# The last group's output in two token halves, its squares on two engines, and the first scores by halves

## The chip, the cores and the metric

The kernel runs on one core of one Trainium2 chip. The metric is the device time of one execution in microseconds; where several runs were made, their median is given. TensorE is the matrix engine, VectorE and ScalarE the two elementwise engines (DVE and ACT in the profile), GpSimd (POOL) issues the transfers that cast or add. "The trace" is the record of every instruction of one profiled execution, and "the profile" what is read from it. Its span, from the first to the last instruction of the program, is some 1.8 us shorter than the device time of the same execution.

## The reference

Four batches of 6080 tokens with 256 channels go through an attention between channels, and the result, 24320 tokens, through two linear layers with a squared relu between them:

```python
def _attn_ref(q, k, v, tau):
    qn = q / (np.linalg.norm(q, axis=1, keepdims=True) + 1e-06)
    kn = k / (np.linalg.norm(k, axis=1, keepdims=True) + 1e-06)
    s = kn.transpose(0, 2, 1) @ qn / tau          # 256 x 256 scores of each batch
    s = s - s.max(-1, keepdims=True)
    a = np.exp(s)
    a /= a.sum(-1, keepdims=True) + 1e-09
    return (v @ a).astype(np.float32)

def _moe_ref(x, w_in, w_out, s, b):               # x: 24320 x 256, d_ff = 2048
    r = np.maximum(x @ w_in, 0.0)
    return ((s * (r * r) + b) @ w_out).astype(np.float32)
```

## The kernel before

The attention matrix is folded into the first layer's weights, batch by batch. So the main stream is: for each group of 512 tokens sixteen steps, each a first-layer product into PSUM; a relu on ScalarE every second step; squares; and the second layer. For most groups the second layer is a scheme of seven products (`seven_items`) on sums S of the squares, run one group behind. The first and the last group use the plain second layer. The last group has 256 tokens, two rows of tokens per partition.

```python
def plain_mm2(g, m):                      # output of one group, slice m of the hidden units
    for h in range((nj + 1) // 2):        # one pass for the last group
        js = [j for j in (2 * h, 2 * h + 1) if j < nj]
        if m == 0:
            o_plain[g, h] = ps_o.tile([P, 2, C], FP32, tag="o_ps", name="o_ps")
        ...                               # for j in js: one matmul of 256 columns
        if m == FT - 1:
            ...
            evacuate(o_sbs[g][:, js[0] : js[-1] + 1, :], o, rowconst, 1)
            if js[-1] == nj - 1:
                store(g)
```

The scores of the first batch are needed before the main stream can start; a softmax without the maximum is taken of their transpose:

```python
po(nc.vector.tensor_mul(                  # recip(): scale by the norms, 512 per partition
    st["s"], self.s_ps, st["r"][:, 1, :, None].broadcast_to((P, CH, C))))
...
for j in range(CH):                       # turn(): four transposes on TensorE
    for ch in range(CH):
        po(nc.tensor.transpose(
            st["t"][:, j, ts(ch, P)], st["s"][:, ch, ts(j, P)], ident32))
```

## Time and profile before

| | before |
|---|---|
| time, median of the first 3 runs | 724.11 us (724.01 to 724.62) |
| span of the profiled run | 722.44 us |
| TensorE, VectorE, ScalarE busy | 97%, 86%, 75% |
| first matmul after the wait for w_in | 40.33 us |
| tail: from the last group's first matmul of 256 columns (703.20) to the end | 19.24 us |

The tail: everything of the change but the first scores lies in it. It starts here (start, length, engine, line, what):

```profile
703.20 0.38 PE L572 MATMUL h_ps<-vT,wa 128*128 128x256 f16 x2
```

The stretches of 0.2 us add what no instruction shows, the data of the last store. The columns are the stretch, its length, busy time of TensorE, its weight loads, VectorE, ScalarE and GpSimd with their instructions, the granted clock, the share of the DMA engines that was busy, and GB/s:

```profile
719.80:720.00 0.20, 0.00 (x0) 0.00 (x0) 0.00 (x0) 0.00 (x0) 0.00 (x0) 1.00 1.07 410
720.20:720.40 0.20, 0.00 (x0) 0.00 (x0) 0.00 (x0) 0.00 (x0) 0.00 (x0) 0.57 0.67 246
```

All engines are idle and the transfer runs at 410 GB/s; with the stretches beside these, it moves data for about 0.8 us (0.82 by the records of its packets).

### The profile page before, as it was taken

How to read it: one execution, taken by the hardware profiler on the slowest of the kernel's cores; microseconds unless marked ns; L12 is line 12 of the kernel's file. 1: busy time of each engine (PE TensorE's matmuls, PEld its weight loads, DVE VectorE, ACT ScalarE, POOL GpSimd, SP SyncE). 2: the span in 40 equal slices, each digit the busy share in tenths (PEclk: the TensorE clock that was granted, in tenths of full speed). 3: DMA queues.
4: the chain of work that ended last, by engine and by line, in shares of the span. 5: the costliest groups of instructions: out<-in, count | busy, mean ns of one | idle time of the engine just before them, and what ended most of it. 6: DMA issues, size and time to landing. Idle time of an engine off the chain costs nothing.

```text
span 722.4 us, 17620 instructions
## 1 busy us (share of the span) xinstructions
PE 700.5 (97%) x7486; PEld 505.8 (70%) x7486; DVE 623.9 (86%) x873; ACT 541.8 (75%) x585; POOL 112.0 (15%) x191
## 2 busy tenths in 40 slices
PE   4799999999999999999999999999999999999997
PEld 2556777766777777777677777777668777777776
DVE  4779999988889999998788999998888888888886
ACT  4479877887777777788777778778777777877772
POOL 4522331211201222111010222111000000000000
PEclk9999999999999999999999999999999999999999
DMA  9999997556465979464863777836323333321201
GB/s 237 209 258 139 176 173 139 95 114 124 97 113 109 157 138 144 101 96 81 149 142 65 138 136 124 152 79 96 96 66 75 93 70 74 100 55 58 70 30 75
DMA packets 86303, 83.83 MB, mean 116 GB/s; under 512 B 56224, under 2 KB 61232, under 8 KB 86224
## 3 DMA queue, kind: packets, MB, share of 16 engines
q0 software_dynamic: 26176, 43.74, 37.6%
q1 hardware_dynamic: 59616, 37.64, 20.9%
q8 instruction: 59, 0.97, 0.6%
q10 hardware_dynamic: 432, 1.31, 0.5%
q14 instruction: 20, 0.16, 0.1%
HBM read 78.91 MB, written 24.90 MB: 144 GB/s over the span
## 4 chain that ended last, share of the span: by engine, by line
PE 88%; DMA 6%; issue 2%; DVE 1%; ACT 1%; POOL 1%; POOLq 0%; ACTq 0%
PE h_ps L572 43%; PE o_ps L716 38%; PE s_ps L142 4%; PE wa_ps L284 2%; DMA qk<-in_q_dram 2%; DMA w_in<-in_moe_w_in_dram 1%; DMA f<-f 1%; DMA qk<-in_k_dram 1%; ACT r L582 1%; PE o_ps L620 1%; POOL qk L126 1%; DVE o_sb L600 0%; DVE S L642 0%; ACT g L593 0%; PE t_ps L247 0%
## 5 line engine op out<-in xcount | busy, mean ns | idle before, releaser
L582 ACT ACTIVATE r<-h_ps 128x1024 f16<-128x1024 f32 (+1 forms) x384 | 387.8, 1013 | 147.6 <-PE h_ps L572 146.0
L572 PE MATMUL h_ps<-vT,wa 128*128 128x512 f16 (+7 forms) x1632 | 452.0, 365 | 0.6 <-ACT r L582 0.4
L716 PEld LDWEIGHTS <-S 128*128 128x128 f16 x2944 | 198.0, 98 | 85.1 <-DVE S L642 0.4
L716 PEld LDWEIGHTS <-g 128*128 128x128 f16 x2208 | 155.1, 98 | 74.1
L595 DVE TENSOR_TENSOR g<-r 128x2048 f16<-128x2048 f16 (+2 forms) x154 | 176.6, 1147 | 16.9 <-ACT r L582 16.5
L716 PE MATMUL o_ps<-T,S 128*128 128x128 f16 x2208 | 183.3, 219 | 0.3 <-DVE S L642 0.2
L572 PEld LDWEIGHTS <-wa 128*128 128x128 f16 x1632 | 136.1, 98 | 21.3 <-issue 1.0
L716 PE MATMUL o_ps<-w_out,g 128*128 128x128 f16 x1472 | 134.3, 219 | 0.3 <-DVE u L600 0.3
L600 DVE SCALAR_TENSOR_TENSOR o_sb<-o_ps,s_out,u 128x256 f32<-128x256 f32 x138 | 66.6, 482 | 50.3 <-PE o_ps L716 48.1
L593 ACT ACTIVATE g<-r 128x1024 f16<-128x1024 f16 x93 | 97.9, 1053 | 0.0
L142 PE MATMUL s_ps<-qk 128*128 128x256 f16 (+1 forms) x384 | 69.6, 281 | 14.5 <-ACT qk L133 7.0
L331 POOL DMA_DIRECT2D v<-in_v_dram x48 | 31.8, 670 | 243.5 <-DMA vT<-v 190.8
L188 POOL DMA_DIRECT2D f<-f x33 | 28.9, 875 | 244.7 <-DVE f L178 191.6
L600 DVE SCALAR_TENSOR_TENSOR u<-o_ps,s_out,rowconst 128x256 f32<-128x256 f32 x138 | 66.1, 479 | 0.5 <-PE o_ps L716 0.5
L716 PE MATMUL o_ps<-N,g 128*128 128x128 f16 x736 | 63.5, 219 | 0.0
L716 PE MATMUL o_ps<-w_out,S 128*128 128x128 f16 x736 | 63.5, 219 | 0.0
L165 ACT ACTIVATE sq<-qk 128x1024 f16<-128x1024 f16 (+3 forms) x49 | 50.4, 1033 | 10.7 <-DMA qk<-in_k_dram 7.5
L644 DVE TENSOR_TENSOR S<-S,g 128x2048 f16<-128x2048 f16 (+1 forms) x47 | 56.5, 1202 | 1.3
L642 DVE TENSOR_TENSOR S<-g 128x2048 f16<-128x2048 f16 (+1 forms) x47 | 56.1, 1193 | 0.0
L648 DVE TENSOR_TENSOR S<-g,S 128x2048 f16<-128x2048 f16 x46 | 56.0, 1218 | 0.0
L646 DVE TENSOR_TENSOR S<-g 128x2048 f16<-128x2048 f16 x46 | 55.9, 1216 | 0.0
L142 PEld LDWEIGHTS <-qk 128*128 128x128 f16 (+1 forms) x384 | 32.6, 101 | 20.2 <-DVE qk L132 8.9
(68 smaller groups left out, 321.8 us busy)
## 6 DMA issues: line engine op xcount, KB each, us to landing
out_dram<-o_sb SPq DMA_DIRECT2D x46, 512.0 KB, 3.1
v<-in_v_dram POOLq DMA_DIRECT2D x47, 256.0 KB, 4.7
qk<-in_k_dram POOLq DMA_DIRECT2D x42, 256.0 KB, 6.0
qk<-in_q_dram POOLq DMA_DIRECT2D x42, 256.0 KB, 7.5
f<-f POOLq DMA_DIRECT2D x30, 128.0 KB, 3.1
vT<-v SPq DMA_TRANSPOSE x182, 3.3
w<-in_moe_w_out_dram POOLq DMA_DIRECT2D x4, 512.0 KB, 11.9
raw<-in_q_dram ACTq DMA_DIRECT2D x2, 512.0 KB, 6.6
```

The source lines that it names most:

```text
L142: po(nc.tensor.matmul(self.s_ps[:, ch, :], kc[:np_, j, ts(ch, P)], qc[:np_, j, :], start=(c == 0 and j == 0 and ch == 0), stop=(c == len(s ...
L165: po(nc.scalar.activation(out=st["sq"][:np_, 1, js, :], in_=kc[:np_, js, :], func=AF.Square))
L572: po(nc.tensor.matmul(dst, wa[:, ci, ts(m, P)], src, start=(ci == 0), stop=(ci == CH - 1), skip_group_check=True))
L582: po(nc.scalar.activation(out=r16[:, :, i % 2, :n], in_=h_tiles.pop((g, i))[:, :, :n], func=AF.Relu))
L593: po(nc.scalar.activation(out=dst, in_=src, func=AF.Square))
L595: po(nc.vector.tensor_mul(dst, src, src))
L600: po(nc.vector.scalar_tensor_tensor(out=dst, in0=src, scalar=s_out, op0=ALU.mult, in1=add, op1=ALU.add))
L642: po(nc.vector.tensor_add(T[1], A21, A22))
L644: po(nc.vector.tensor_sub(T[2], T[1], A11))
L646: po(nc.vector.tensor_sub(T[3], A11, A21))
L648: po(nc.vector.tensor_sub(T[4], A12, T[2]))
L716: po(nc.tensor.matmul(st[name][:, j, :], a()[:, i, ts(j, P)], w[:, i, :], start=first, stop=last, skip_group_check=True))
```

## The change

Its intent is to shorten the end. The last group's output is computed for one half of the tokens first, so that this half's eviction and store lie under the other half's matmuls, and only half an eviction and half a store follow the last matmul. ScalarE takes every second square, to relieve VectorE. At the start, the first scores are scaled in two pieces, so that TensorE can turn the first piece early. The core of the diff:

```diff
-                po(nc.vector.tensor_mul(
-                    st["s"], self.s_ps, st["r"][:, 1, :, None].broadcast_to((P, CH, C))))
+                if self.b == 0:
+                    for ch in range(CH):
+                        po(nc.vector.tensor_scalar_mul(
+                            out=st["s"][:, ch], in0=self.s_ps[:, ch],
+                            scalar1=st["r"][:, 1, ch : ch + 1]))
+                else:
+                    ...                       # as before
@@ turn()
-                for j in range(CH):
-                    for ch in range(CH):
+                for ch in range(CH):
+                    for j in range(CH):
@@
+    def last_mm2(j, m):
+        g = NG - 1
+        if m == 0:
+            o_plain[g, j] = ps_o.tile([P, 2, C], FP32, tag="o_ps", name="o_ps")
+        o = o_plain[g, j][:, 0:1, :]
+        ...                                   # one matmul of 256 columns
+        if m == FT - 1:
+            ...
+            po(nc.vector.scalar_tensor_tensor(
+                out=o_sbs[g][:, j, :], in0=o[:, 0, :], scalar=s_out, op0=ALU.mult,
+                in1=rowconst, op1=ALU.add))
+            store(g, j, j + 1 if j == 0 else None)
@@ plain_mm2
+        if g == NG - 1:
+            last_mm2(0, m)
+            if m == FT - 1:
+                for i in range(FT):
+                    last_mm2(1, i)
+            return
@@ main loop, plain groups
-                square(g, m // 2, m // 2 + 1, nc.vector)
+                late = g > 0 and m // 2 % 2 == 1
+                square(g, m // 2, m // 2 + 1, nc.scalar if late else nc.vector)
```

More of the change, by code (lines that the diff above doesn't have):

```diff
@@ L239, in recip @@
                 st["s"] = sm_pool.tile([P, CH, C], FP32, tag="sm_s", name="sm_s")
-                po(nc.vector.tensor_mul(
-                    st["s"], self.s_ps, st["r"][:, 1, :, None].broadcast_to((P, CH, C))))
+                if self.b == 0:
[4 more added lines that the diff above has]
+                else:
+                    po(nc.vector.tensor_mul(
+                        st["s"], self.s_ps, st["r"][:, 1, :, None].broadcast_to((P, CH, C))))
             def turn():
                 st["t"] = self.bank("t_ps", CH, C)
-                for j in range(CH):
-                    for ch in range(CH):
+                for ch in range(CH):
+                    for j in range(CH):
                         po(nc.tensor.transpose(
@@ L609, in store @@
             in_=o_sb[:, j0:j1, :]))
+    def last_mm2(j, m):
+        g = NG - 1
+        assert group(g)[1] == 2
+        if m == 0:
+            o_plain[g, j] = ps_o.tile([P, 2, C], FP32, tag="o_ps", name="o_ps")
+        o = o_plain[g, j][:, 0:1, :]
+        po(nc.tensor.matmul(o[:, 0, :], g_tiles[g][:, m % 2, m // 2, ts(j, P)],
+                            w_out16[:, m, :], start=(m == 0), stop=(m == FT - 1),
+                            skip_group_check=True))
+        if m == FT - 1:
+            if j == 0:
+                o_sbs[g] = opool.tile([P, TG // P, C], FP32, tag="o_sb", name="o_sb")
+            po(nc.vector.scalar_tensor_tensor(
+                out=o_sbs[g][:, j, :], in0=o[:, 0, :], scalar=s_out, op0=ALU.mult,
+                in1=rowconst, op1=ALU.add))
+            store(g, j, j + 1 if j == 0 else None)
     def plain_mm2(g, m):
         _, nj = group(g)
+        if g == NG - 1:
[4 more added lines that the diff above has]
+            return
         for h in range((nj + 1) // 2):
```

## The prediction

> **What bounds the kernel now.** I read the page first (shares by engine, then the 40 slices), then the chain that ended last, and then only the two short stretches that the change touches: 35 to 42 us, where the first scores are scaled, and 703 us to the end, the last group of 256 tokens.
>
> ```profile
> PE 700.5 (97%) x7486; PEld 505.8 (70%) x7486; DVE 623.9 (86%) x873; ACT 541.8 (75%) x585; POOL 112.0 (15%) x191
> PE   4799999999999999999999999999999999999997
> ...
> PE 88%; DMA 6%; issue 2%; DVE 1%; ACT 1%; POOL 1%; POOLq 0%; ACTq 0%
> ```
>
> TensorE is full from the fourth slice to the last and makes 88% of the chain. Nothing in the change takes a matmul out: it can only move waits, and the few microseconds at each end when TensorE is not the bound. The chain of waits, around the first scores and at the end:
>
> ```profile
> 30.04 10.25 DMA w_in<-in_moe_w_in_dram
> 40.28 0.05 issue
> 40.33 1.04 PE wa_ps L284 x4
> ...
> 707.62 0.45 PE o_ps L716 x8
> 708.07 0.22 PE o_ps L620 x2
> 708.29 0.22 PE h_ps L572 x2
> 708.51 0.55 PE o_ps L716 x8
> 709.06 0.22 PE o_ps L620 x2
> 709.27 0.22 PE h_ps L572 x2
> 709.49 0.52 PE o_ps L716 x8
> ...
> 716.86 1.11 PE o_ps L620 x10
> 717.96 0.02 issue
> 717.99 0.75 DVE o_sb L600
> ```
>
> Columns are start, length, what. To be seen: the chain passes from the load of w_in (10.25 us) straight to a matmul at 40.33, so the scaling and turning of the scores at 36 to 37.5 us is not on it. In the last group one step is 0.22 (first layer, two matmuls of 256 columns) + 0.45 (eight products of the group before) + 0.22 (output, two matmuls) = 0.88 us; only two steps are longer, by 0.10 and 0.07. Then ten output matmuls, one eviction of 0.75 us and a store. The timeline of the tail and of the scores:
>
> ```profile
> 36.02 0.69 DVE L240 TENSOR_TENSOR sm_s<-s_ps,rnrm 128x512 f32<-128x512 f32 x1
> 36.85 0.63 PE L247 MATMUL t_ps<-ident,sm_s 128*128 128x128 f32 x4 [0.16 <-DVE sm_s L240]
> 37.52 0.84 ACT L257 ACTIVATE eT<-t_ps,rnrm 128x256 f16<-128x256 f32 x2 [0.53 <-PE t_ps L247]
> ...
> 715.78 0.60 ACT L582 ACTIVATE r<-h_ps 128x512 f16<-128x512 f32 x1 [1.17 <-PE h_ps L572]
> 716.41 0.42 DVE L595 TENSOR_TENSOR g<-r 128x512 f16<-128x512 f16 x1 [0.58 <-ACT r L582]
> 716.89 0.48 DVE L600 SCALAR_TENSOR_TENSOR o_sb<-o_ps,s_out,rowconst 128x256 f32<-128x256 f32 x1
> 717.99 0.75 DVE L600 SCALAR_TENSOR_TENSOR o_sb<-o_ps,s_out,rowconst 128x512 f32<-128x512 f32 x1 [0.61 <-PE o_ps L620]
> 718.77 0.35 ACTq L607 DMA_DIRECT2D out_dram<-o_sb  x1
> ```
>
> After 718.77 no compute engine works. The stretches of 0.2 us show the last store's data moving from about 719.6 to 720.4 (297, 410, 358, 246 GB/s); the span ends at 722.4, some 2 us later.
>
> **What the Trainium skill says.** (1) "TensorE: Matmul & The Clock Gate", section Back-to-back issue gap: 256 columns take 262 cycles at 2.4 GHz, an estimate from it of 109 ns. The trace agrees: 0.22 us for two, 1.11 for ten. (2) "ScalarE: Activation LUTs", section What ACT_TABLE_LOAD costs: 186 ns + 0.833 ns per element with immediate scale, about 93 ns of it overlapped by the next. For 512 elements that is 612 ns; the trace has 594 as the mean of the 128x512 relu, so I take 0.60 us for a square on ScalarE. (3) "VectorE: DVE Perf Modes", section The TRN2 errata: a fixed extra cost per instruction, so small tiles pay relatively more. The trace agrees: the eviction costs 0.48 us for 256 elements and 0.75 for 512, not half. (4) "DMA: Bandwidth & Descriptors", section Latency and other measured facts: a DMA has a fixed cost of about 2 us, dominated by the receipt from memory. The last store landed 2.1 us after issue, about 0.8 of it data.
>
> **The change part by part.**
> *First scores by halves.* One 0.69 us multiply becomes two on 256 elements. The 256-element PSUM multiply on VectorE elsewhere in this stretch took 0.48 us, and one such instruction starts about 0.40 after another (evictions at 698 to 717 us). So the first half is ready at 36.02 + 0.48 = 36.50, the second at 36.02 + 0.40 + 0.48 = 36.90 (now 36.71). Five filler matmuls hold TensorE to about 36.53. With the lag of 0.14 us now seen, the first two turns start at 36.64, the last two at 37.04, and the last ends near 37.43 in place of 37.48. The exponentials gain 0.05 us; but at 40.33 TensorE waits for w_in with 0.16 us of idle time before it, so this gain is swallowed: 0.
>
> *Squares shared.* Eight squares of 128x512 on VectorE (0.42 us each, 0.33 start to start) become four there and four on ScalarE (0.60 us). ScalarE idles 1.17 us in nearly every pair of steps, so it has room. VectorE is freed of 4 x 0.33 = 1.3 us of its queue. Its queue is what made the two long steps: the partial sums S for the other group's products (ending 709.33) and the eviction that frees a bank (ending 708.39) are followed 0.06 us later by the products at 709.39 and 708.45. Without the square at 706.98 both come 0.33 us earlier: 709.00 and 708.06.
>
> *Two halves.* The number and width of matmuls are the same, 32 of 256 columns. Before the end, each step now has one output matmul, not two, so a step is 0.77 us and TensorE asks earlier. I step through it. Step 7's products would start at 708.45 - 0.10 - 2 x 0.11 = 708.12; the bank is free at 708.06 + 0.06 = 708.12: no wait. Step 8's would start at 708.89, the sums come at 709.06: a wait of 0.17. Steps 9 to 12 find their inputs (the third sums are ready at 710.53, wanted at 711.36). Step 13's are wanted at 712.90; VectorE's fourth sums end at 712.86, so about 0.02. Step 15 starts at 714.24, the last group's products end at 715.44.
>
> Then comes the new end. The five remaining matmuls of the first half start at 715.44; the fourth needs the last square. Last first-layer result 714.62, relu 714.66 to 715.26, square on ScalarE 715.30 to 715.90, seen at 715.96, wanted at 715.77: a wait of 0.19. The second half takes a new PSUM tile. Of the three buffers of that pool, two hold the other group's accumulators and one the first half, so it must take the oldest accumulator, which VectorE evicts from 715.64 to 716.12: free at 716.18, just when the first half's last matmul has been issued (715.96 + 0.22). No further wait. Sixteen matmuls of 0.108 end issuing at 717.91 and, with the drain of 0.17 seen now, finish at 718.08, against 717.95 now. So the waits rise from 0.17 to about 0.38 us; the extra 0.2, less rounding, costs about 0.13.
>
> What is won is behind it. The last eviction is 0.48 in place of 0.75: -0.27. The first half's eviction and store lie under the second half's 1.7 us of matmuls. The last store is 128 KB, not 256: at the 410 GB/s seen, 0.64 us of data becomes 0.32; with rows of 1 KB rather than 2 KB a little of it is lost (packet records of the trace: 4 KB 160 ns, 2 KB 86 ns, so by straight line 49 ns for 1 KB, and 8 x 37 = 0.30 us saved per queue engine). The fixed receipt stays. Sum: 0 + 0.13 - 0.27 - 0.30 = -0.44, rounded to -0.5 since the waits at 709 and 715.8 are worked from rounded lags and may be smaller. 724.11 - 0.5 gives 723.6 us.
>
> **The rivals.** (a) *The waits are larger*: the square on ScalarE lies on the way to the end (it is 0.18 us longer than on VectorE), and the second half's tile waits for an eviction. If either slips by some 0.4 us, the gain is eaten: 724.1. For it: the three-buffer pool and the serial relu, square, matmul; against it: both releases fall within 0.2 us of their need in my working. (b) *The waits vanish*: VectorE, relieved, delivers its sums in time, and the 0.17 us of old waits go without new ones; then the end is at 717.8 and the whole is -0.9: 723.2. For it: 1.3 us of VectorE time freed; against it: TensorE's demand moves up by 0.11 a step as well. (c) *The store is all fixed cost*: only the eviction counts and the total is -0.1: 724.0. Against it: data was seen moving for 0.8 us. (d) *The start counts*: if the w_in load lands earlier in most runs than in the profiled one, the scores would be on the path, worth 0.05 us or, if the second half's later multiply dominates, costing as little. Not seen in this trace.
>
> **Range and chances.** The rivals lie between 723.2 and 724.1; the three runs before spread over 0.6 us, and loads at the start vary from run to run. I give 722.9 to 724.3. 2% is 14.5 us; the whole stretch after the last group's start is 19 us and nearly all of it matmuls, so neither verdict beyond 2% is plausible: 0.005 faster, 0.985 within, 0.01 slower.
>
> **What would show it.** In the new profile: TensorE's matmul after the w_in load still near 40.3 with slightly more idle time before it; in the last group, output matmuls one at a time with steps of 0.77 us, four 128x512 squares of about 0.6 us on ScalarE, the long step at 709.06; a gap of about 0.2 us before the fourth of the first half's last five; sixteen output matmuls ending near 718.1; a final eviction of 0.48 us; and last store data lasting about 0.4 us. Wrong would be: a shift of the matmul at 40.3 us by more than 0.2, any change between 60 and 700 us (there is no changed instruction there), a gap over 0.5 us before the second half, or an end that does not move though the eviction and the store shrank.

## More of the kernel before

The experiments ran in sets, on two chips; times are compared only within a set.

For the batches after the first, the squares of q and k that make the norms are folded per chunk, and each chunk's fold is added to the first chunk's by an accumulating transfer. Matmuls with ones then sum over the partitions; their result shares a PSUM bank with an accumulator of the second layer.

```python
def into_first():
    dst, src = self.rows[0][0][:np_], st["f", 1][:np_]
    po(nc.gpsimd.dma_start(out=dst, in_=src, accum_op=ALU.add))
```

## The result, and the profile after

The changed kernel took 724.26 us (723.56 to 724.57, 6 runs), the kernel before 724.44 us (724.01 to 725.0, 6 runs). The ratio is 0.9996, with a 95% interval of 0.9983 to 1.0009: the same. Ratios here are the mean time of one kernel's runs over that of the other's of the same rounds, so not quite the ratio of the quoted medians. All runs with rounds were fast ones, the granted clock 0.998 to 1.0.

Seen from the time, the change did next to nothing. The trace says otherwise.

**The start.** The timeline of the changed kernel:

```profile
35.82 0.87 DVE L242 TENSOR_SCALAR sm_s<-s_ps,rnrm 128x256 f32<-128x256 f32 x2
36.45 0.74 PE L253 MATMUL t_ps<-ident,sm_s 128*128 128x128 f32 x4
37.23 0.84 ACT L263 ACTIVATE eT<-t_ps,rnrm 128x256 f16<-128x256 f32 x2 [0.43 <-PE t_ps L253]
40.13 1.04 PE L290 MATMUL wa_ps<-w_in,eT 128*128 128x512 f16 x4 [0.24 <-DMA w_in<-in_moe_w_in_dram]
```

From the start of the scaling to the exponentials are 37.23 - 35.82 = 1.41 us; before they were 37.52 - 36.02 = 1.50. So 0.09 us was won, and at the matmul that needs w_in it became idle time: 0.24 us in place of 0.16.

**The tail.** The chain of waits in the last group, and at its end (start, length, what):

```profile
708.65 0.45 PE o_ps L746 x8
709.09 0.11 PE o_ps L624
709.20 0.22 PE h_ps L578 x2
709.42 0.61 PE o_ps L746 x8
...
716.36 2.15 PE o_ps L624 x18
718.54 0.48 DVE o_sb L630
```

Each step has one output matmul of 0.11 us, so a step is 0.77 us. One long step (0.61 in place of 0.45) is left where there were two. The gap before the eighteen last matmuls, and what stands behind it, is in the timeline of the tail:

```profile
715.05 0.60 ACT L588 ACTIVATE r<-h_ps 128x512 f16<-128x512 f32 x1 [0.96 <-PE h_ps L578]
715.68 0.63 ACT L599 ACTIVATE g<-r 128x512 f16<-128x512 f16 x1
716.05 0.48 DVE L606 SCALAR_TENSOR_TENSOR o_sb<-o_ps,s_out,rowconst 128x256 f32<-128x256 f32 x1 [0.85 <-PE o_ps L746]
717.31 2.10 ACTq L613 DMA_DIRECT2D out_dram<-o_sb  x2
```

and it starts with

```profile
703.56 0.38 PE L578 MATMUL h_ps<-vT,wa 128*128 128x256 f16 x2
```

The last square ends at 716.31 and the fourth of the first half's last five matmuls starts at 716.36: 0.293 us after the third, where 0.109 is the spacing, so a wait of 0.18. The tail runs from 703.56 to 722.31, 18.75 us: 0.49 less than before. Counted from the tail's start, the final eviction begins at 14.98 us (14.79 before), so +0.19; it takes 0.48 in place of 0.75, -0.27; and from the last store's issue (0.35 us before 719.41, where the two issues end) to the end are 3.25 us in place of 3.67, -0.42. The sum is -0.50. The stretches of 0.2 us show the shorter store: only these two carry more than 102 GB/s, where before there were four.

```profile
720.00:720.20 0.20, 0.00 (x0) 0.00 (x0) 0.00 (x0) 0.00 (x0) 0.00 (x0) 1.00 1.06 358
720.20:720.40 0.20, 0.00 (x0) 0.00 (x0) 0.00 (x0) 0.00 (x0) 0.00 (x0) 1.00 0.60 195
```

**Where the half microsecond went.** Laying the matmuls of the two traces beside each other, one by one in their order, shows one place between the start and the tail where they part: near 150 us, at the matmuls that sum the second batch's norms. The chains of waits there, before:

```profile
144.67 5.24 DMA f<-f
...
150.04 0.24 PE o_ps L217 x4
```

and after:

```profile
144.47 5.78 DMA f<-f
...
150.38 0.24 PE o_ps L217 x4
```

The same accumulating transfer, issued 0.20 us earlier, took 0.54 us longer to land. TensorE waits for it in both kernels. No instruction near it was changed. So either such a landing varies by itself and hid the gain, or the change costs something there; the experiments had to tell.

### The profile page after: what moved, and what is told of

Its sections match the earlier page's. It is cut to its first block, busy times and chain, and to the rows that moved or that the text cites. A ratio compares the mean times of both kernels' runs of the same rounds, so it can differ in the third digit from the quotient of the medians.

```text
span 722.3 us, 17624 instructions
## 1 busy us (share of the span) xinstructions
PE 700.6 (97%) x7486; PEld 505.6 (70%) x7486; DVE 623.0 (86%) x871; ACT 544.8 (75%) x589; POOL 112.5 (16%) x191
## 4 chain that ended last, share of the span: by engine, by line
PE 89%; DMA 6%; issue 2%; DVE 1%; ACT 1%; POOL 1%; POOLq 0%; ACTq 0%
PE h_ps L578 43%; PE o_ps L746 38%; PE s_ps L142 4%; DMA qk<-in_q_dram 2%; PE wa_ps L290 2%; DMA f<-f 1%; DMA w_in<-in_moe_w_in_dram 1%; DMA qk<-in_k_dram 1%; ACT r L588 1%; POOL qk L126 1%; PE o_ps L624 1%; PE o_ps L650 0%; DVE S L672 0%; ACT g L599 0%; DVE o_sb L606 0%
## 5 line engine op out<-in xcount | busy, mean ns | idle before, releaser
L601 DVE TENSOR_TENSOR g<-r 128x2048 f16<-128x2048 f16 (+2 forms) x150 | 174.7, 1164 | 16.5 <-ACT r L588 16.2
L599 ACT ACTIVATE g<-r 128x1024 f16<-128x1024 f16 (+1 forms) x97 | 100.4, 1035 | 0.2
```

Of the source, the lines that this page charges most:

```text
L599: po(nc.scalar.activation(out=dst, in_=src, func=AF.Square))
L601: po(nc.vector.tensor_mul(dst, src, src))
```

## The experiments

Theory H (hidden gain): the tail is 0.5 us shorter, always; what hides it are two landings that vary from run to run, that of w_in near 40 us and that of the accumulating transfer near 150 us. Rival R: the change itself costs as much elsewhere, near 150 us or at the start. Smaller questions: which part of the change earns the 0.5 us, and whether the wait that it made can be taken away.

### The kernel before once more, and the changed one once more

No edit. `null` is the kernel before.

> The kernel before once more, as a control. The theory that the change is worth 0.5 us at the end but is hidden by a landing time that varies says: ratio to before 1.000 within the interval, single runs spread over 0.5 to 1 us, and the wait of TensorE for the norms of the second batch near 150 us differs from the profile of before (where it was 0.9 us) by tenths of a us. The tail, from the first 256-column first-layer matmul to the end of the span, is 19.24 us again within 0.1. The rival, that times repeat to 0.1 us and the changed kernel lost 0.5 us elsewhere because of the change, says: the wait near 150 us is 0.9 us again.

> The changed kernel once more. Hidden-gain theory: tail 18.74 us again within 0.1 (0.5 below before); the wait near 150 us takes some new value between 0.8 and 1.7 us; ratio between 0.9985 and 1.0. Rival (the change costs 0.5 us near 150 us): the wait is 1.4 us again and the ratio is 1.000.

`null` took 724.30 us (723.83 to 724.53), the changed kernel 724.38 (724.14 to 724.51), the kernel before of the same rounds 724.14 (723.73 to 724.72, 9 runs); ratios 1.0001 and 1.0002. Tails: 19.24 and 18.76 us. From the traces, with "gap" for the time between the starts of the two matmuls around the wait near 150 us (0.06 us without a wait):

| kernel | matmul after w_in | gap near 150 us | tail | span | rest |
|---|---|---|---|---|---|
| before | 40.33 | 1.13 | 19.24 | 722.44 | 661.74 |
| null | 40.19 | 1.25 | 19.24 | 722.44 | 661.76 |
| after | 40.13 | 1.67 | 18.75 | 722.31 | 661.76 |
| after_again | 40.60 | 1.28 | 18.76 | 722.41 | 661.77 |
| halves_only (below) | 40.20 | 1.42 | 19.12 | 722.49 | 661.75 |
| one_store (below) | 40.26 | 1.45 | 19.18 | 722.63 | 661.74 |
| last_dve (below) | 40.51 | 0.68 | 18.54 | 721.48 | 661.75 |

The rest is the span less the three. It agrees to 0.03 us over seven traces of five different kernels: the three terms are the whole difference between any two of these executions. The tail belongs to the kernel and repeats to 0.01 us. The other two vary by 0.47 and 0.99 us, and the three other traces with the changed code of these stretches have gaps of 0.68, 1.28 and 1.45. The gap is 1.27 us on average in these four with the change at the start, and 1.26 in the three without it, so the traces show no cost near 150 us. The two terms are not independent: the transfer is issued 104.34 us after the w_in matmul in every trace, so a late start shortens the gap, and their sum varies by 0.69 us. These timed runs gave the changed kernel no gain, so R at the start was not out: its w_in matmul came at 40.60.

### Norms later: the wait taken away, clumsily

```diff
-    FIN = (-12, 0, 3, 3, 6, 8, 10, 13)
+    FIN = (-12, 3, 6, 6, 9, 11, 13, 16)
```

The norms and all that follows them come three steps later in batches two to four, in the kernel before and in the changed one.

> The kernel before with the norms and all that follows them in later batches three steps later, so that TensorE asks for the accumulated squares some 2.5 us after it does now. If the varying landing of the third accumulating transfer is what sets the run-to-run spread: no wait for it near 150 us, the time falls by the wait, 0.9 to 1.4 us, to about 723.2 (ratio near 0.9985), and single runs lie within 0.5 us. If the spread has another source: the time falls by about as much but the spread stays at 1 us. If the wait only moves: no change.

> The same on the changed kernel. Hidden-gain theory: 0.5 us below the run before with the late norms, so about 722.7 us, ratio near 0.9977, and tail 18.74. Rival: equal to the kernel before with late norms within 0.2 us.

Measured: 724.89 us (724.68 to 725.00) and 724.71 us (724.64 to 724.84); ratios 1.0009 and 1.0007. Both medians are above that of the kernel before (724.14), though the intervals begin at 0.9997 and 0.9994, and the spread of single runs fell to 0.32 and 0.20 us. The wait for the transfer is gone (gap 0.06), but in each of the three batches two new waits came. The chain of waits of the first, in `before_late`:

```profile
151.97 0.18 ACT nrm L228
...
152.19 0.49 PE o_ps L716 x6
```

Three steps later the square root on ScalarE stands behind a relu, and the bank it reads is wanted by a product. So the expected time was missed; the point about the spread held. The tails are 19.23 and 18.75 us, but the medians differ by 0.18 us, the means by 0.14, and not by 0.5. In the two traces, each of the first run of its set, the w_in matmul came at 40.12 and at 40.51, which gives back 0.39. Since the other four runs of each set lie so near the first, what gave it back acted in nearly all of them: it was no chance of single runs. R at the start had to be tried by itself.

### A quiet base, and each part on it

Only the norms of the second batch go two steps later:

```diff
+                d = 2 if i == 1 and gr.b == 1 else 0
-                at_step(int(s) + 1 + (FIN[i] if i < 8 else FIN[7] + 3 + (i - 8) * 3), f)
+                at_step(int(s) + 1 + d + (FIN[i] if i < 8 else FIN[7] + 3 + (i - 8) * 3), f)
```

Four kernels on this base, run on one chip: without the change, with the first scores by halves alone, with the last group's part alone, and with the whole change.

> The kernel before with only the norms of the second batch two steps later (a base without the wait of 1.0 to 1.6 us near 150 us, and without the new waits that the three-step shift of everything brought). Expected: no wait near 150 us, 723.2 us (724.2 less 1.0), spread of single runs at most 0.5 us.

> The quiet base with the first scores alone scaled and turned by halves. Theory that this part is neutral (prediction): equal to quiet_before within 0.1 us. Rival, raised by the last four runs: scaling by halves delays the landing of w_in that starts the main stream, by 0.3 us: 0.3 us above quiet_before, and the matmul after the w_in wait at 40.5 rather than 40.2 us.

> The quiet base with the last group's halves and shared squares alone. Both theories: tail 18.74 us against 19.24. Neutral-scores theory: 0.5 us below quiet_before and equal to quiet_after. Rival: 0.5 below quiet_before and 0.3 below quiet_after.

> The quiet base with the whole change. Neutral-scores theory: 0.5 us below quiet_before, near 722.7. Rival (scores cost 0.3): 0.2 us below quiet_before.

| on the quiet base | median of 5 | range | ratio to before | matmul after w_in | tail |
|---|---|---|---|---|---|
| without the change | 723.76 | 723.41 to 723.92 | 0.9988 | 40.47 | 19.24 |
| first scores alone | 723.71 | 723.43 to 723.98 | 0.9989 | 40.66 | 19.22 |
| last group alone | 723.19 | 722.96 to 723.46 | 0.9982 | 40.52 | 18.76 |
| whole change | 723.14 | 722.98 to 723.24 | 0.9981 | 40.42 | 18.75 |

The kernel before of the same rounds took 724.36 us (723.81 to 724.89, 8 runs). On a base whose runs lie within 0.3 to 0.6 us of each other the whole change is worth 723.76 - 723.14 = 0.62 us, the last group alone 0.57, and the first scores 0.05. Between the means the whole change is worth 0.54 us, and the last group's part 0.51 over the ten runs with it and the ten without. The ranges of the kernels with and without the last group's part overlap by 0.05 us (723.41 to 723.46). H holds for the size of the gain, and R at the start falls in this set: the first scores are neutral within what these runs can tell. R near 150 us can't be tried here, since the base takes that wait away; against it stand the equal mean gaps above. The base won 0.6 us and not 1.0, since a shorter wait (gap 0.56) took the old one's place. Its chain of waits:

```profile
150.82 0.41 DVE u L601
...
151.27 0.24 PE o_ps L217 x4
```

The norms now wait for the eviction of the accumulator whose bank they share, and no transfer stands in the chain.

### The halves without the shared squares

```diff
-                late = g > 0 and m // 2 % 2 == 1
-                square(g, m // 2, m // 2 + 1, nc.scalar if late else nc.vector)
+                square(g, m // 2, m // 2 + 1, nc.vector)
```

The first scores are also as before here.

> The kernel before with the last group's output in two halves, but all its squares on VectorE. If the shared squares are what pays for the halves: VectorE's sums and evictions come as late as before while TensorE asks earlier, waits grow by about 0.6 us and the tail is 19.3 us, no shorter than before (19.24). If the squares are incidental: tail 18.6 to 18.8 us as in the changed kernel.

One look (a single run, so its state is unknown; the tail is read within its trace): 724.26 us, tail 19.12 us. So the halves alone win 0.12 us, not 0.49, and the shared squares, added to them, the other 0.37. What the shared squares would win without the halves was not run. The chain of waits shows why:

```profile
711.75 0.33 DVE g L595
712.08 0.39 DVE o_sb L600
712.48 1.14 DVE S L672
...
713.66 0.62 PE o_ps L740 x8
```

From 707.2 to 713.6 us the chain runs on VectorE (squares g, sums S, evictions), and TensorE waits three times. With one output matmul a step in place of two, TensorE asks faster than VectorE can deliver. I had expected 0.6 us of added waits; the last matmul started 0.57 us later in the tail than before (15.04 against 14.47), and the shorter eviction and store gave back 0.69.

### One store in place of two

```diff
-            store(g, j, j + 1 if j == 0 else None)
+            if j == 1:
+                store(g)
```

> The changed kernel with one store of both halves (256 KB) at the end in place of two. If the shorter last transfer gives 0.3 to 0.4 us: tail 19.1 to 19.15 us. If a store's end is fixed cost: 18.74.

724.40 us; tail 19.18 us, 0.43 more than with two stores. The timeline has one issue:

```profile
718.94 0.36 ACTq L613 DMA_DIRECT2D out_dram<-o_sb  x1
```

From here to the end of the span (722.63) are 3.69 us, as in the kernel before. So two stores in place of one are worth 0.43 us, and without them nearly the whole gain is gone. From the issue to the landing this store took 2.08 us and the smaller one of the changed kernel 1.73; the rest, 0.09, lies after the landing (see the store below).

### The last square back on VectorE

```diff
-                late = g > 0 and m // 2 % 2 == 1
+                late = g > 0 and m // 2 in (1, 3, 5)
```

> The changed kernel with the last of the eight squares back on VectorE. If the wait of 0.18 us before the fourth of the first half's last five matmuls comes from ScalarE's longer square alone and nothing stands behind it: tail 18.56 us. If, as the prediction has it, the second half's bank is freed at just that time (eviction ending 16.53 - 0.56 us into the tail, in the profile 716.53): the wait moves to the first matmul of the second half and the tail stays 18.74 within 0.05.

723.25 us; tail 18.54 us, 0.20 less than in the changed kernel. The wait is gone and nothing took its place. The timeline:

```profile
715.23 2.46 PE L624 MATMUL o_ps<-w_out,g 128*128 128x256 f16 x21
715.43 0.48 DVE L606 SCALAR_TENSOR_TENSOR o_sb<-o_ps,s_out,rowconst 128x256 f32<-128x256 f32 x1
```

Twenty-one matmuls run without a gap. The sixth, the second half's first, starts at 715.23 + 5 x 0.109 = 715.77, while the oldest accumulator is still being evicted until 715.91. So the second half's tile does not lie in that bank. The pool's other accumulator had been evicted at 714.58. (This run's short time of 723.25 us is mostly luck: its gap near 150 us was 0.68.)

### A version to beat both

On the changed kernel: the last square on VectorE; the second half's output in the idle bank of the gram pool (needless, as `last_dve` shows); and the last chunk's folded squares of the second batch go to the norms by four more matmuls, so that no transfer is waited for.

```diff
+            direct = self.b == 1 and c == len(self.chunks) - 1
-                    if last and (self.b == 0 or c == 0):
+                    if last and (self.b == 0 or c == 0 or direct):
-            return ops + [into_first] if self.b > 0 and c > 0 else ops
+            return ops + [into_first] if self.b > 0 and c > 0 and not direct else ops
```

> A version to beat both: the changed kernel; the last square back on VectorE and the second half's output in the idle bank of the gram pool, which takes both causes of the 0.18 us wait away (tail 18.56); and the last chunk's squares of the second batch given to the norms directly, by four more matmuls, in place of the accumulating transfer that is waited for near 150 us (1.0 to 1.6 us less, 0.24 us of matmuls more). Expected: no wait for a transfer near 150 us, 722.5 us, ratio near 0.9975, runs within 0.5 us of each other.

Measured: 722.52 us (722.30 to 722.70), the kernel before of the same rounds 724.69 (723.86 to 725.50, 9 runs), ratio 0.997 with an interval of 0.9957 to 0.9984. The tail is 18.55 us. The timeline near 150 us has the norms' eight matmuls in the stream, with no idle time ahead of them:

```profile
148.84 0.34 PE L218 MATMUL o_ps<-ones,f 128*128 128x1 f16 x8
```

Single runs lie within 0.40 us of each other, while those of the kernel before on the same chip spread over 1.64 us. So both the wait and most of the scatter came from that one transfer; the other two ways of not waiting for it gave small spreads too (0.20 to 0.32 us and 0.26 to 0.55). All twelve kernels gave correct results.

## Why the prediction was right or wrong

The predicted time was 723.6 us in a range of 722.9 to 724.3; measured were 724.26 us, inside, but 0.04 us from the edge. A change of -0.5 us was expected; the first rounds showed -0.18 between the medians, the quiet base -0.62. That the number fell in the range is partly luck: it was counted from 724.11, the median of three runs, and six runs of the same kernel gave 724.44. One of its own signs of being wrong came true: any change between 60 and 700 us was to count, and 0.54 us came near 150. Another was met to the limit: the w_in matmul moved by 0.20 us, where more than 0.2 was to count, and by 0.27 in `after_again`. Neither sign allowed for a landing that varies.

- **First scores by halves: right.** 0 expected. The second multiply started 0.40 us after the first, as expected. The exponentials gained 0.09 us (0.05 expected) and the wait for w_in took it; 0.05 us between medians on the quiet base. Over all traces, the w_in matmul came at 40.31 us on average in the six without this part and at 40.41 in the eight with it, over a range of 0.5 us: no effect can be told from the scatter.
- **Squares shared: right, and with the halves the larger part of the gain.** The wait at step 7 went, that at step 8 stayed at 0.15 us (0.17 expected). `halves_only` shows that 0.37 us of the 0.49 is lost without this. In the kernel before, the two waits add up to only 0.17 us; with the halves alone the three add up to 0.72. A square on ScalarE took 0.63 us, not 0.60.
- **The wait for the last square: right.** 0.18 us measured, 0.19 expected, and `last_dve` took it away by its cause.
- **The second half's bank: wrong.** The step said that the tile "must take the oldest accumulator", freed just in time. `last_dve` started the second half 0.14 us before that eviction ended. The error cost nothing in the sum, as the wait before it was as long, but by it moving the last square back would have won nothing, and it won 0.20 us.
- **The eviction: right**, -0.27. **The store: right, and a term was missing.** Its data shrank from 0.82 to 0.52 us, as worked out, and the time from issue to landing from 2.06 to 1.73, -0.33 where -0.30 was expected. The other -0.09 lies after the landing. In the traces SyncE waits at the end for one semaphore after another. With two stores the first one's semaphore has been passed long before the last lands, so one such wait fewer follows: from the landing to the end are 1.59 to 1.61 us in the six traces with one store at the end, 1.52 in the eight with two.
- **The sum of the tail: right, in part by luck.** -0.44 before rounding, -0.49 measured. The waits cost 0.19 us and not 0.13, the end after the last eviction won 0.42 and not 0.30, and the two errors have opposite signs.
- **"Range and chances": the step that failed.** It names loads at the start as what varies and counts the first three runs' 0.6 us as the noise. The wait for an accumulating transfer near 150 us, 0.9 us in the waits of before, stands in the same chain of waits and was not looked at, as no changed line is near it. It alone varied by 0.99 us from trace to trace, twice the gain, and no term of the prediction stands for it. Of the rivals, none of the four names it.

What stays open: in the first two sets of rounds and in the pair with late norms the gain was between 0.3 and -0.1 us by the means, less than the traces' terms would give on average. Only one run of a set left a trace, so I can't show whether the landings of the others fell badly for the changed kernel or something else took part; the pair with late norms speaks for something that stays the same through a set.

Why these landings vary is open too, but for the accumulating transfer the traces show where. Of the batch's four accumulating transfers in the kernel before, two with no packets of other queues beside them landed in 2.71 and 2.76 us, and one beside 0.36 MB of them in 3.15. The last took 5.24 beside 0.59 MB: a store of 512 KB is issued 0.12 us after it, and transposes follow. Its own data had ended 0.81 us before the landing, and this stretch was 1.26 us in the changed kernel and 0.48 in `last_dve`. Over the thirteen traces with this transfer it varied by 0.89 us, the time from the issue to the last data by 0.33. So what varies most is the time from its last data to its landing, under traffic of others. No run moved that store, so that it is the cause is not shown.

## What to carry to other kernels

To judge a gain well below the scatter of runs, find a stretch that repeats within one trace, and account for the rest of the span in terms: here one remainder agreed to 0.03 us over seven traces, which told how much lay in the tail and how much in two landings outside it. Then take the scatter away at its cause: the wait for one transfer was worth more than the change that was being judged. And where a stage is split so that one engine asks faster, relieve the engine that feeds it in the same change; the halves alone won 0.12 us, with the shared squares 0.49.

## What the Trainium skill lacked or had wrong

- "DMA: Bandwidth & Descriptors", section Latency and other measured facts, gives a fixed cost of about 2 us. The last stores of the fourteen traces landed 1.73 to 2.08 us after issue, with 0.51 to 0.83 us of data, so their fixed part was 1.2 to 1.3 us.
- The same section has the fixed cost grow with the load on HBM, but gives no spread for one transfer that shares the engines with others. Here the accumulating transfer of 112 KB took 5.24 and 5.78 us in two executions with the same neighbours, and the median of all such transfers was 3.1 us. None of the pages read says that one landing can set the run-to-run scatter of a kernel.
- "VectorE: DVE Perf Modes", section The TRN2 errata, gives 120 + 256 cycles at 0.96 GHz for 256 fp32 elements from PSUM, an estimate of 392 ns. The instruction behind such an eviction did start 0.40 us after it (the middle of 255 cases), but the eviction, as recorded, took 0.48, and that is what the end of a chain pays. (The prediction rests on the section's statement of a fixed extra cost per instruction; the section makes it of sources in SBUF, and the evictions read PSUM, for which this formula stands.)
